# Attention into a SwiGLU block: q transposed in 32x32 blocks on VectorE, its loads in quarters of the partitions

## The chip, the cores and the metric

The kernel runs on one core of a Trainium2 chip. The metric is the device time of one execution in microseconds (us). The time before is the median of five runs, 1066.11 us (1065.39 to 1068.65). Traces come from the hardware profiler, one execution each.

The engines are TensorE (PE, matrix products and transposes through an identity), VectorE (DVE), ScalarE (ACT), GpSimd (POOL) and SyncE (SP), which in this kernel issues nearly all DMAs. SBUF has 128 partitions; PE writes to PSUM.

## The reference

```python
# q, k, v: (8, 8, 576, 64) = (batch B, head H, position S, D)
kv = np.einsum('bhsd,bhse->bhde', k, v)          # no softmax: one 64x64 matrix per head
out = np.einsum('bhsd,bhde->bhse', q, kv)
rms = np.sqrt(np.mean(out * out, axis=-1, keepdims=True) + 1e-06)
attn = out / rms * g_norm
x = attn.transpose(0, 2, 1, 3).reshape(4608, 512)
g = x @ w_gate                                     # (512, 1536)
h = g * (1.0 / (1.0 + np.exp(-g))) * (x @ w_val)
y = h @ w_out                                      # (1536, 512)
```

## The kernel before

The 4608 tokens are worked in nine blocks of 512 (NB = 9, BLK = 512, four tiles of 128). Block n ends batch n-1 and begins batch n, since a batch has 576 positions. `Att` holds the attention part of a block, `Ffn` the rest.

Attention. `load_kv` (L223) loads k and v for pairs of heads j = 0 to 3; `kv` (L255) multiplies them on PE, and one ACT copy (L261) and one DVE add make the 64x64 matrices of the batch. `load_q` (L238) loads two of the block's token tiles at a time with the tokens in the partitions: per partition eight runs, one for each head, of 64 numbers, 256 bytes. PE needs q with the head's dimension in the partitions, so `turn_q` transposes each tile in four 128x128 transposes on PE (L272) into PSUM, and ACT (L274) or DVE (L276) copies them out to `qt`: 16 transposes and four copies for each block. `product` (L292) multiplies qt by the kv matrices; `root` and `scale` do the norm, `turn_x` (L339) transposes the result, and `sums` makes the sums of its quarters (x and, from block 2 on, xi).

The FFN's products are done in the Strassen-Winograd manner, with seven products in place of eight, here in chains that accumulate in the PSUM tiles a, b and c. Block 0 is computed plainly (L861), since weights still arrive. Block 1 does one level in its up phase (`Up`, PE at L427). Blocks from DEEP = 2 on do two levels in the up phase (`Inner`, PE at L576), in 12 units; after nearly every product DVE adds the PSUM tile into a ring tile (L110), and at the end of four units h = silu(g) * v is made (L112, on POOL or, for the last, DVE). The down phase (`Down`, PE at L427) has one level: chains p = 1, 5, 6, 7, 2, 4, 3, each of 12 matmuls of 256 columns (two records each in the trace). Between two levels stand combined weights, which DVE makes in block 1 (`leaf_steps`); SP stores them to memory (L707 and L711, w<-r, w<-t, w<-xi), and streams them back in 51 chunks for each later block (`Stream.pump`, L655, t<-w) into a pool of nine tiles t.

The main loop runs, for each n: the up phase of block n, with the attention loads and kv products of block n+1 as fills between its units; `turn`, the transposes of q of block n+1; the first kv loads of block n+2; and the down phase, between whose products the steps of the attention of block n+1 (`half`, `turn_x`, `sums`) stand. The order of instructions on each engine comes from a scheduler that follows this order and the waits for tiles; pools of few buffers (ld four, t nine, ring r five, xi one, PSUM a one, b three, c two, m two) decide when a tile is free. The last up unit's product and the first Down product meet at the turn, where the transposes stand.

Two names recur: a deep block is one with n >= 2, and the seam is the place between its up and its down phase. All loads and stores named here go through SP's one queue, in order.

Of the kernel before, what the change touches and what calls it, by code (L numbers as in the profile page):

```python
# [8 lines left out]
F32 = mybir.dt.float32  # L9
# [5 lines left out]
P = 128  # L15
# [3 lines left out]
def kernel(  # L19
# [41 lines left out]
    nc = tc.nc  # L61

    B, H, S, D = q.shape
    NT, DM = out.shape
    FF = moe_w_gate.shape[1]
    T = 4
    BLK = P * T
# [3 lines left out]
    NS = DM // P  # L71
# [7 lines left out]
    def pool(name, bufs, **kw):  # L79
        return ctx.enter_context(tc.tile_pool(name=name, bufs=bufs, **kw))  # L80

    consts = pool("consts", 1)
    ld_pool = pool("ld", 4)
# [30 lines left out]
    def ring():  # L114

        return r_pool.tile([P, 4, BLK], F32, name="r")
# [67 lines left out]
    class Att:  # L184
# [29 lines left out]
        def load_kv(self, js):  # L214
            if self.n == B:
                return
            for j in js:
                hs = slice(2 * j, 2 * j + 2)
                for i, (tiles, src) in enumerate(((self.k, k), (self.v, v))):
# [6 lines left out]
                        )  # L226
                    tiles.append(t.rearrange("p h (t d) -> p h t d", t=KT))

        def load_q(self, i):
            if self.n == 1:  # L230
                tiles = [t_tile().rearrange("p a b -> p (a b)") for _ in range(2)]
            else:
                ld = ld_pool.tile([P, 2 * BLK], F32, name="ld")
                tiles = [ld[:, 0:BLK], ld[:, BLK : 2 * BLK]]
            for t in range(2):
                tile_ = tiles[t].rearrange("p (h d) -> p h d", h=H)
                for b, s0, p0, p1 in self.parts(2 * i + t):
                    nc.sync.dma_start(  # L238
                        out=tile_[p0:p1], in_=q[b, :, s0 : s0 + p1 - p0, :].rearrange("h p d -> p h d")
                    )  # L240
                self.q.append(tile_.rearrange("p (j u) d -> p j (u d)", u=2))
# [22 lines left out]
        def turn_q(self, i, pools=None):  # L264

            if i == 0:
                self.qt = ring().rearrange("p t (j c) -> p t j c", j=NS)
            for t in (2 * i, 2 * i + 1):
                pool = pools[t % 2] if pools else m_psum
                ps = pool.tile([P, NS, P], F32, name=pool.name[0])  # L270
                for j in range(NS):
                    nc.tensor.transpose(ps[:, j], self.q[t][:, j], ident)  # L272
                if t % 2 or self.n == 1 or self.n > DEEP:
                    nc.scalar.copy(out=self.qt[:, t], in_=ps)  # L274
                else:
                    nc.vector.tensor_copy(out=self.qt[:, t], in_=ps)  # L276
# [131 lines left out]
    DEEP = 2  # L408
# [261 lines left out]
    def t_tile(key=None):  # L670

        stream.held.append(key)
        return t_pool.tile([P, 2, 2 * P], F32, name="t")
# [206 lines left out]
    def weights(upto):  # L880
        nonlocal loaded, rounded
        while rounded < min(upto, len(pieces)):
            while loaded < min(rounded + 4, len(pieces)):
                load_w(*pieces[loaded])
                loaded += 1
            round_w(*pieces[rounded])
            rounded += 1

    def t2(place, b22, b11):

        sub(nc.vector, place, b22, place)
        add(nc.vector, place, place, b11)

    blocks = [Att(n) for n in range(NB)]
# [7 lines left out]
    for n in range(NB):  # L902
        ffn = Ffn(n, blocks[n])
        nxt = blocks[n + 1] if n + 1 < NB else None
        if n == 0:

            with tc.issue_after(scaled.ins):
                weights(2)
            ffn.plain_up(0, (0,))
            scaled = blocks[0].second()  # L910
            for f in range(NF):
                with tc.issue_after(scaled.ins):
                    weights(2 * (f + 2))
                if f == 1:
                    ffn.plain_up(1, (0,))
                    ffn.plain_up(0, (1,))
                ffn.plain_up(f, (1,)) if f == 1 else ffn.plain_up(f) if f else None
            weights(len(pieces))
            pairs = wo.rearrange("p (j e) d -> p e j d", e=2)
            t2(pairs[:, 0, :, HD:DM], pairs[:, 1, :, HD:DM], pairs[:, 0, :, 0:HD])  # L920
            nxt.room = x_pool.tile([P, 3, 7, P], F32, name="xi").rearrange("p a b c -> p (a b c)")
            nxt.load_kv(range(NS))
            for i in range(2):
                nxt.load_q(i)
            ffn.plain_end()
            nxt.kv(range(NS))
        else:

            def third():
                nxt.kv((0, 1))  # L930
                nxt.load_kv((2, 3))

            def two_thirds():
                nxt.kv((2, 3))
                for i in range(2):
                    nxt.load_q(i)

            ffn.up({4: third, 8: two_thirds} if nxt else {})
        if nxt:
            nxt.turn()  # L940
        if n + 2 < NB:
            blocks[n + 2].load_kv((0, 1))
        ffn.down(nxt.steps() if nxt else [])
        if n == 0:

            with tc.issue_after(nxt.halves[0].ins):
                for j in range(NP):
                    t2(wv[j][:, 0:2], wv[j][:, 2:4], wg[j][:, 0:2])
# [31 lines left out]
```

## Time and profile before

| | us |
|---|---|
| median of five runs | 1066.11 |
| lowest and highest | 1065.39, 1068.65 |
| profiled execution, its own time | 1068.65 |
| span of its trace | 1066.7 |
| PE busy in the span | 1040.1 (98%) |
| DVE busy | 699.0 (66%) |
| POOL busy | 366.4 (34%) |
| ACT busy | 244.9 (23%) |
| start of one deep down phase to the next | 111.76 |
| mean granted PE clock | 0.994 of full speed |

The span reaches from the first to the last instruction that the trace shows; 1.95 us of the profiled execution lie around it. Busy times of different engines overlap. In a line of the trace, `b<-x,t` says that the tile b is written from x and t, `x8` counts instructions, the first number is the start from the span's start and the second the time that the group takes; what stands in brackets is the idle time before it, and who ended it. Instructions of a group may overlap their neighbours, as PE's records are longer than their spacing. A row that ends in `383/622/3250` gives the least, median and most of a duration in ns, followed by the first and last start.

### The profile page before, as it was taken

To read this page: it belongs to the slowest core of one execution; us is meant where nothing else is said; L and a number is where in the kernel's file an instruction comes from. 1 tells how busy PE (TensorE), PEld (TensorE's weight loads), DVE (VectorE), ACT (ScalarE), POOL (GpSimd) and SP (SyncE) were. 2 spreads that over 40 slices of the span, in tenths; PEclk is the share of its full clock that TensorE was granted. 3 is DMA by queue.
4 is the path that set the end of the run, shared out by engine and by line. 5 is a ranking of instruction groups with operands and counts; after the bars stand their busy time and mean duration, and the time that the engine had idled before them with its cause. 6 is when DMAs were issued, how large, how long until landed. Compare 5 with 4: busy or idle time off the path is not lost.

```text
span 1066.7 us, 21799 instructions
## 1 busy us (share of the span) xinstructions
PE 1040.1 (98%) x8780; PEld 937.3 (88%) x8780; DVE 699.0 (66%) x1243; ACT 244.9 (23%) x392; POOL 366.4 (34%) x280
## 2 busy tenths in 40 slices
PE   5899999998999999999999999999999999999998
PEld 4644788877899989998999899989999899989997
DVE  2999596778556765576666666666667566755661
ACT  2666111221221211222112212121112211212110
POOL 0000453344025701462156305640455036602670
PEclk9999999998999999999999999999999999999999
DMA  9787103565468325741576247714782266126611
GB/s 239 221 265 231 57 12 105 160 172 162 158 209 240 112 71 193 238 147 61 163 244 169 83 128 229 220 53 129 225 230 70 90 202 189 50 80 202 189 31 40
DMA packets 154356, 161.87 MB, mean 152 GB/s; under 512 B 48400, under 2 KB 105104, under 8 KB 154256
## 3 DMA queue, kind: packets, MB, share of 16 engines
q1 hardware_dynamic: 154192, 160.48, 50.2%
q8 instruction: 70, 1.15, 0.5%
q14 instruction: 30, 0.25, 0.1%
q0 software_dynamic: 64, 0.00, 0.0%
HBM read 138.02 MB, written 22.41 MB: 150 GB/s over the span
## 4 chain that ended last, share of the span: by engine, by line
PE 92%; DVE 3%; DMA 2%; SPq 2%; POOL 1%; issue 1%; ACT 0%; DVEq 0%; POOLq 0%
PE b L576 25%; PE b L427 20%; PE c L576 12%; PE c L427 10%; PE a L576 6%; PE a L427 5%; PE c L861 4%; PE b L861 4%; PE m L255 2%; PE m L339 1%; PE m L292 1%; SPq L223 1%; PE b L292 1%; DVE r L111 1%; DMA ld<-in_moe_w_gate_dram 1%; PE b L272 1%
## 5 line engine op out<-in xcount | busy, mean ns | idle before, releaser
L110 POOL TENSOR_TENSOR r<-r 128x256 f32<-128x256 f32 (+1 forms) x105 | 110.2, 1055 | 365.7 <-DVE r L110 360.4
L110 DVE TENSOR_TENSOR r<-b,r 128x512 f32<-128x512 f32 (+1 forms) x273 | 162.1, 607 | 61.4 <-PE b L576 56.6
L110 DVE TENSOR_TENSOR r<-c,r 128x512 f32<-128x512 f32 (+1 forms) x177 | 108.9, 625 | 99.4 <-PE c L576 56.0
L111 POOL TENSOR_TENSOR t<-wo 128x512 f32<-128x512 f32 x81 | 113.1, 1423 | 162.1 <-DVE wo L110 108.4
L576 PE MATMUL b<-x,t 128*128 128x128 f32 x1092 | 151.2, 276 | 0.0
L576 PEld LDWEIGHTS b<-x,t 128*128 128x128 f32 x1092 | 136.0, 192 | 0.6
L110 DVE TENSOR_TENSOR r<-a,r 128x512 f32<-128x512 f32 (+1 forms) x99 | 62.6, 632 | 83.2 <-PE a L576 53.1
L112 POOL TENSOR_TENSOR h<-r 128x1024 f32<-128x1024 f32 (+1 forms) x40 | 81.5, 2053 | 93.2 <-DVE r L110 79.7
L576 PE MATMUL c<-xi,t 128*128 128x128 f32 x840 | 112.1, 275 | 0.0
L576 PEld LDWEIGHTS c<-xi,t 128*128 128x128 f32 x840 | 102.8, 192 | 0.0
L427 PE MATMUL b<-t,h 128*128 128x256 f32 x432 | 97.1, 381 | 0.0
L427 PE MATMUL b<-wo,h 128*128 128x256 f32 x432 | 96.2, 379 | 0.0
L427 PEld LDWEIGHTS b<-wo,h 128*128 128x128 f32 x432 | 81.4, 190 | 10.7
L427 PEld LDWEIGHTS b<-t,h 128*128 128x128 f32 x432 | 80.7, 190 | 11.0 <-issue 0.2
L590 ACT COPY r<-b 128x512 f32<-128x512 f32 x63 | 36.9, 586 | 219.1 <-PE b L576 184.9
L576 PE MATMUL b<-xi,t 128*128 128x128 f32 x588 | 79.7, 276 | 0.0
L576 PEld LDWEIGHTS b<-xi,t 128*128 128x128 f32 x588 | 72.4, 192 | 0.0
L576 PE MATMUL b<-x,wg 128*128 128x128 f32 x336 | 53.0, 280 | 0.0
L576 PE MATMUL b<-x,wv 128*128 128x128 f32 x336 | 51.2, 275 | 0.0
L427 PE MATMUL c<-t,s 128*128 128x256 f32 x216 | 48.9, 383 | 0.0
L427 PE MATMUL a<-wo,h 128*128 128x256 f32 x216 | 48.3, 379 | 0.0
L427 PE MATMUL c<-wo,h 128*128 128x256 f32 x216 | 48.1, 379 | 0.0
(129 smaller groups left out, 1649.8 us busy)
## 6 DMA issues: line engine op xcount, KB each, us to landing
t<-w SPq DMA_DIRECT2D x336, 256.0 KB, 2.9
out_dram<-r SPq DMA_DIRECT2D x18, 512.0 KB, 2.9
ld<-in_q_dram SPq DMA_DIRECT2D x29, 256.0 KB, 4.5
ld<-in_moe_w_gate_dram SPq DMA_DIRECT2D x12, 512.0 KB, 4.9
ld<-in_moe_w_val_dram SPq DMA_DIRECT2D x12, 512.0 KB, 5.1
ld<-in_moe_w_out_dram SPq DMA_DIRECT2D x12, 512.0 KB, 4.6
w<-t SPq DMA_DIRECT2D x36, 128.0 KB, 2.1
ld<-in_k_dram SPq DMA_DIRECT2D x26, 160.0 KB, 3.1
```

Source lines behind the costliest of these rows:

```text
L110: add = lambda e, o, a, b: e.tensor_tensor(out=o, in0=a, in1=b, op=OP.add)
L111: sub = lambda e, o, a, b: e.tensor_tensor(out=o, in0=a, in1=b, op=OP.subtract)
L112: mul = lambda e, o, a, b: e.tensor_tensor(out=o, in0=a, in1=b, op=OP.mult)
L223: nc.sync.dma_start(out=t[r * D : (r + 1) * D, :, 0 : m * D], in_=src[self.n, hs, s0 : s0 + m * D].rearrange("h (p t) d -> p h (t d)", t=m),)
L255: nc.tensor.matmul(self.kv_ps[r][u * D : (u + 1) * D, j, :], lhsT=self.k[j][rows, u, c, :], rhs=self.v[j][rows, u, c, :], start=(c == 0), ...
L272: nc.tensor.transpose(ps[:, j], self.q[t][:, j], ident)
L292: nc.tensor.matmul(self.ps[i][u][p : p + D, t, j, :], lhsT=self.qt[rows, 2 * i + t, j, p : p + D], rhs=kvs[b % 3][rows, j, :], start=True, ...
L339: nc.tensor.transpose(ps[:, e, t], xt[:, t, j + e], ident)
L427: nc.tensor.matmul(self.ps[name][:, e], lhsT=lhsT, rhs=rhs, start=first and (e, i) == (0, 0), stop=i == self.steps - 1, skip_group_check=True,
L576: nc.tensor.matmul(ps[:, i, f], lhsT=self.weight(o, p, f), rhs=self.operand(o, p), start=first and (i, f) == (0, 0), stop=True, skip_group ...
L590: nc.scalar.copy(out=dst, in_=ps)
L861: nc.tensor.matmul(t, lhsT=w[f // 2][:, i, P * (f % 2) : P * (f % 2 + 1)], rhs=x[:, i, of], start=(i == 0), stop=(i == NS - 1),)
```

## The change

For blocks from 2 on, q is loaded by a new function, `load_quarters`: for each pair of token tiles, each j of two and each quarter r of the partitions it loads 32 positions in 32 partitions by as many groups of 32 positions as belong to one batch, 32 numbers (128 bytes) to a run. A block's q takes 32 DMAs where it took four or five (16 where block 8 has one batch alone). `turn_q` then transposes in two VectorE instructions of 128x1024, which turn each 32x32 block in place, straight from SBUF to SBUF: with quarters of the columns in quarters of the partitions, that is the whole transpose. Sixteen PE transposes and four copies out of PSUM fall away per turn. qt lies in its ring tile in another order of dimensions. Blocks 0 and 1 keep PE transposes.

The loads of q of block n+2 move to the start of the down phase of block n, beside the first kv load. k and v are loaded and multiplied one j at a time, at units 2, 5, 8 and 11 of the up phase (2, 4, 8, 10 in block 1), where they were loaded and multiplied two at a time at 4 and 8; only the first j is loaded in the down phase before.

```diff
--- before.py
+++ after.py
@@ -226,7 +226,30 @@
                         )
                     tiles.append(t.rearrange("p h (t d) -> p h t d", t=KT))
 
+        def load_quarters(self, i):
+
+
+            ld = ld_pool.tile([P, 2 * BLK], F32, name="ld")
+            to = ld.rearrange("p (j g d) -> p j g d", j=2, d=P // 4)
+            cut = 2 * self.n
+            spans = [(self.n - 1, S - D * self.n, 0, cut), (self.n, 0, cut, BLK // 32)]
+            for j in range(2):
+                for r in range(4):
+                    h, d = divmod(r, 2)
+                    for b, s0, g0, g1 in spans:
+                        if g1 > g0:
+                            nc.sync.dma_start(
+                                out=to[32 * r : 32 * (r + 1), j, g0:g1],
+                                in_=q[b, 4 * i + 2 * j + h, s0 : s0 + 32 * (g1 - g0), 32 * d : 32 * (d + 1)].rearrange(
+                                    "(g p) d -> p g d", p=32
+                                ),
+                            )
+            self.q.append(ld)
+
         def load_q(self, i):
+            if self.n >= DEEP:
+                self.load_quarters(i)
+                return
             if self.n == 1:
                 tiles = [t_tile().rearrange("p a b -> p (a b)") for _ in range(2)]
             else:
@@ -264,13 +287,17 @@
         def turn_q(self, i, pools=None):
 
             if i == 0:
-                self.qt = ring().rearrange("p t (j c) -> p t j c", j=NS)
+                self.qt = ring().rearrange("p j (t c) -> p t j c", t=T)
+            if self.n >= DEEP:
+                to = self.qt[:, :, 2 * i : 2 * i + 2].rearrange("p t j c -> p j t c")
+                nc.vector.transpose(out=to.rearrange("p j t c -> p (j t c)"), in_=self.q[i])
+                return
             for t in (2 * i, 2 * i + 1):
                 pool = pools[t % 2] if pools else m_psum
                 ps = pool.tile([P, NS, P], F32, name=pool.name[0])
                 for j in range(NS):
                     nc.tensor.transpose(ps[:, j], self.q[t][:, j], ident)
-                if t % 2 or self.n == 1 or self.n > DEEP:
+                if t % 2 or self.n == 1:
                     nc.scalar.copy(out=self.qt[:, t], in_=ps)
                 else:
                     nc.vector.tensor_copy(out=self.qt[:, t], in_=ps)
@@ -926,20 +953,19 @@
             nxt.kv(range(NS))
         else:
 
-            def third():
-                nxt.kv((0, 1))
-                nxt.load_kv((2, 3))
-
-            def two_thirds():
-                nxt.kv((2, 3))
-                for i in range(2):
-                    nxt.load_q(i)
-
-            ffn.up({4: third, 8: two_thirds} if nxt else {})
+            def fill(j):
+                nxt.kv((j,))
+                if j + 1 < NS:
+                    nxt.load_kv((j + 1,))
+
+            at = (2, 5, 8, 11) if n >= DEEP else (2, 4, 8, 10)
+            ffn.up({a: (lambda j=j: fill(j)) for j, a in enumerate(at)} if nxt else {})
         if nxt:
             nxt.turn()
         if n + 2 < NB:
-            blocks[n + 2].load_kv((0, 1))
+            blocks[n + 2].load_kv((0,))
+            for i in range(2):
+                blocks[n + 2].load_q(i)
         ffn.down(nxt.steps() if nxt else [])
         if n == 0:
 
```

## The prediction

> **What bounds the kernel now.** I read the page's busy shares and the chain that ended last first:
>
> ```profile
> PE 1040.1 (98%) x8780; PEld 937.3 (88%) x8780; DVE 699.0 (66%) x1243; ACT 244.9 (23%) x392; POOL 366.4 (34%) x280
> PE 92%; DVE 3%; DMA 2%; SPq 2%; POOL 1%; issue 1%; ACT 0%; DVEq 0%; POOLq 0%
> ```
>
> TensorE is the bound, so work taken off it is worth its time, unless another engine then ends last. Next I looked at the place where the transposes stand, the turn from up to down of a deep block (n = 3 here; blocks follow each other every 111.76 us), on PE and on VectorE:
>
> ```profile
> 471.74 1.16 PE L576 MATMUL b<-x,t 128*128 128x128 f32 x8
> 472.73 0.60 PE L272 MATMUL m<-ident,ld 128*128 128x128 f32 x4
> 473.17 0.60 PE L272 MATMUL b<-ident,ld 128*128 128x128 f32 x4
> 473.61 0.60 PE L272 MATMUL m<-ident,ld 128*128 128x128 f32 x4
> 474.04 0.60 PE L272 MATMUL b<-ident,ld 128*128 128x128 f32 x4
> ...
> 472.99 0.69 DVE L110 TENSOR_TENSOR r<-b,r 128x512 f32<-128x512 f32 x1 [0.41 <-PE b L576]
> 473.78 2.52 DVE L112 TENSOR_TENSOR h<-r 128x1024 f32<-128x1024 f32 x2
> ```
>
> The 16 transposes occupy PE from 472.73 to 474.48 (start of the first Down product), 1.75 us, without a gap. Beside them DVE makes the last add and the last two products of h. How full both are, by windows (columns: PE, PEld, DVE, ACT and POOL busy, clock, DMA share, GB/s):
>
> ```profile
> 463.70:470.00 6.30, 6.30 (x58) 6.30 (x58) 4.91 (x10) 1.06 (x1) 5.15 (x6) 1.00 0.33 102
> 470.00:474.64 4.64, 4.64 (x42) 4.56 (x41) 3.62 (x5) 1.22 (x2) 2.33 (x1) 1.00 0.01 4
> 474.64:515.00 40.36, 40.36 (x311) 35.38 (x310) 26.93 (x46) 8.74 (x16) 8.91 (x6) 1.00 0.27 87
> 228.00:248.00 20.00, 15.70 (x57) 13.06 (x58) 14.30 (x35) 4.24 (x8) 5.33 (x5) 0.78 0.54 156
> ```
>
> PE has no idle time in the deep block and DVE has some. The last row is block 1, where the combined weights are also made: PE idles there at a lowered clock. Last, SyncE's queue at the end of block 1 and in a deep down phase:
>
> ```profile
> 272.61 2.87 SPq L711 DMA_DIRECT2D w<-xi  x3
> ...
> 473.80 1.25 SPq L223 DMA_DIRECT2D ld<-in_k_dram  x2
> 482.91 27.98 SPq L655 DMA_DIRECT2D t<-w  x9
> ```
>
> In block 1, SP issues its stores of weights back to back until 275.48; in a deep block it mostly waits for tiles.
>
> **PE transposes out: gain 10.5 us.** Seven turns lose 16 transposes each. Six stand in deep blocks (n = 2 to 7): 6 x 1.75 = 10.5 us, if the work behind can start that much sooner. The seventh (block 2's q, in block 1) has 6 of its 16 just before a PE gap of 3.38 us (ended by ACT); only the ten at 249.87 to 250.96, 1.1 us, lie on the path.
>
> **What is late next at the seam.** Down's p = 1 product has 12 matmuls of 0.432 us (24 records 0.216 apart); its last four need the last h. In the changed program the scheduler puts three Down matmuls ahead of the last Up group, so that group, its add and the h products move back by 3 x 0.432 = 1.30. The first h product then ends at 473.78 + 1.30 + 1.22 = 476.30; PE, free of transposes, reaches the ninth Down matmul at 474.48 + 8 x 0.432 - 1.75 = 476.19. It waits 0.11, six times.
>
> **VectorE transposes in: no gain; 1.5 us lost with the seam's wait, up to 15 us.** Fourteen new DVE instructions, two per turn, 128x1024 each, ten and four adds ahead of the h products. No row shows this operation. The nearest has the same shape and memory, 128x1024 f32 read and written in SBUF: 1.225 us (L112). Two take 2.45. The kv add, now at the eleventh unit instead of the eighth, joins them: 0.42 by the 128x256 adds, and DVE waits for an ACT copy ahead of it:
>
> ```profile
> DVE kv L110 <- ACT kv L261: 5.2, 5, 1.0
> ```
>
> That is 1.0 each. Queued behind both are the adds of the last units, and PE waits for these through the PSUM tiles that they free. So DVE gets 2.45 + 0.42 + 1.0 = 3.87 us more, and has 1.39 + 1.02 idle from 463.7 to 474.64 and the 1.30 by which the last group moves back, 3.71. It is short by 0.16; with the 0.11 above, 0.25 per seam (rounded), six times 1.5 us. There is no margin left: each 0.1 us by which a transpose exceeds 1.225 costs 6 x 2 x 0.1 = 1.2 us, a doubled one (2.45) 14.7. Below 1.225 at most the 1.5 come back. I take 1.225, as the nearest row. The evictions that go (26 on ACT of 0.59, 2 on DVE of 0.68) are beside the path. The first qt product, which reads the result, starts after the first Down chain.
>
> The Trainium skill ("Vector Engine (DVE) Microarchitecture Reference", section 3.8) has the 32x32 transpose sustain one element per cycle and lane; no run here shows it yet, and by it the price would be near the row's.
>
> **The loads on SP: between 0 and +12 us, taken +4.8, once.** q of blocks 2 to 8 now takes 32 DMAs per block (16 for block 8) of 32 partitions and 128-byte runs instead of 4 or 5: 177 more on SP. What an issue takes now (least, median and most, in ns):
>
> ```profile
> L238 SPq DMA_DIRECT2D ld<-in_q_dram x35: 383/622/3250, 0.7 to 800.6; - x35
> L223 SPq DMA_DIRECT2D ld<-in_k_dram x52: 595/602/1265, 98.9 to 764.2; - x52
> ```
>
> The least of L238 is that of 128 partitions, 0.383; L223's 0.602 is for 64 partitions, in steps of 0.67 with the gap. Thirty-two partitions are not shown; the nearest is 64, so 0.67 a step, 32 x 0.67 = 21.4 us per block. From below, 128 partitions give 0.43 a step; from above, if the halving again adds 0.22, 0.89. Each load also waits for the landing of the one eight before it: at 4.5 us to landing (the page's median for q), 0.56 a step at the least, so this wait is covered.
> - Deep blocks: issued after the remaining kv loads, from about 475 on, they end at 496.5. Queued behind them are the t<-w loads, 9 before the next up phase at 515.52 (9 x 0.37 = 3.3 us of issue and 2.9 to land), and stores at 511.15. That is late only if a step exceeds (515.52 - 6.2 - 475.1) / 32 = 1.07 us. Cost 0.
> - Block 1: block 3's 32 loads come ahead of the last 32 weight stores on a queue without air. They add 21.4, less four q(2) DMAs that move into down of block 0 (2.94) and four kv DMAs that move to later fills (2.7): 15.8 us. The last store is issued at 291.3 instead of 275.48 and lands 2.1 later, 293.4. Block 2's xi sums, whose tile these stores read, began at 286.01 and now wait for it; they last 4.34 and end at 297.7. PE first reads xi at 292.89: 4.8 us late. The 1.1 us of PE time saved and DVE's extra (2 x 1.225 - 2 x 0.685 = 1.1) in this block vanish in that wait. At 0.43 a step it is nothing, at 0.89 it is 12; each 0.05 is 1.6 us.
> - Bytes are unchanged and runs halve. When q is loaded now, with 256-byte runs, and when the weights stream, with 2 KB:
>
> ```profile
> 451.00:452.00 1.00, 1.00 (x11) 1.00 (x10) 0.21 (x1) 0.48 (x1) 0.00 (x0) 1.00 1.05 226
> 457.00:458.00 1.00, 1.00 (x11) 1.00 (x11) 0.69 (x1) 0.00 (x0) 1.00 (x1) 1.00 1.02 387
> ```
>
> If the rate halves again to 113 GB/s, a block's 1.05 MB takes 9.3 us, in a down phase where the DMA share is 0.27 of 40 us. Cost 0; moving it out of the full stretch of the up phase, where PE does not wait, gains 0.
>
> The rule that speaks against it is in the Trainium skill, "DMA: Bandwidth & Descriptors", Specifications: below 512 B a transfer is a read-modify-write and misses line rate. The two windows agree for 256 B (226 against 387 GB/s); by the rule the change is a loss on the queue's engines, by the windows one that nobody waits for.
>
> **kv one pair of heads at a time** (units 2, 5, 8, 11): the same matmuls and DMAs in smaller portions. Cost 0 on PE; its add is counted above.
>
> **Sum.** -10.5 + 1.5 + 4.8 = -4.2 us. The profiled execution took 1068.65 (span 1066.7 and 1.95 around it), the highest of five; so 1064.4 against it, and 1061.9 against the median, 1066.1, by which I state the numbers. About 0.2% (2.1 us) is what a measurement of this kernel can tell from no change.
>
> **Rivals.**
> - *Dear issues on SP.* A step of 32 partitions is over 0.75, say 0.9 to 1.1 us. For it: 64 partitions cost 0.22 more than 128. Against: the 64-partition loads of q and kv cost much the same though their runs differ, so a fixed price is as likely as a rising one. Block 1 then loses 12 to 18.5: -9.0 + 12 = +3 to -9.0 + 18.5 = +9.5, 1069 to 1075.6. It decides for slower from 0.80 a step (-9.0 + 4.8 + 32 x 0.13 = 0). Chance 0.27.
> - *Dear transposes on VectorE.* Over 1.4 us, say 2.45: -4.2 + 14.7 = +10.5, 1076.6; slower from 1.225 + 4.2 / 12 = 1.58. Against it is the equal shape of L112. Chance 0.12.
> - *The seam keeps the time.* Down's h ends last at the turn whatever PE does (today DVE ends it at 476.30, 1.8 us after PE has started Down), and PE waits for it. Half the gain stays: -5.25 + 4.8, about -0.4, 1065.7. Against it: today PE needs the last h only at 474.48 + 8 x 0.432 = 477.94. Chance 0.11.
> - *Forecast*, with a step of 0.43 to 0.75: -9.0 + 0 to -9.0 + 7.4, 1057.1 to 1064.5. Chance 0.50.
>
> **Numbers.** Forecast, SP, DVE and seam in this order: faster 0.46 + 0 + 0.03 + 0.04 = 0.53; same 0.04 + 0.07 + 0.02 + 0.05 = 0.18; slower 0 + 0.20 + 0.07 + 0.02 = 0.29. The range reaches down to the whole 10.5 with nothing given back, and up to a step of 1.05 (-4.2 + 32 x 0.38 = +8): 1055.5 to 1074.
>
> **What would show it.** Right: deep turns 1.5 us shorter (period about 110.3), no PE gap over 0.3 us at the first Down chain, DVE transposes of about 1.2 us, SP issues of about 0.6, and block 2's xi sums waiting for a w store until about 293. Wrong: transposes above 1.5 us, issues above 0.8 with block 2's up phase after 300, a deep up phase that waits for t<-w, or PE waiting for kv or q products.

## The result and the profile after

The changed kernel takes 1068.06 us (median of 23 runs, 1067.37 to 1070.80), against 1066.58 us before (median of 43): ratio 1.0019, 95% interval 1.0013 to 1.0024. It is slightly slower, where 1061.9 was forecast. Its profiled execution took 1069.35 us, its span is 1067.6. In the runs below, each ratio is against the kernel before on the same chip in the same rounds; the one profiled execution of a version differs from its median by up to 3.5 us (e6_kv_pairs), so stages are compared by traces and versions by ratios.

The page's busy shares, and the chain that ended last, after:

```profile
PE 1033.2 (97%) x8668; PEld 924.0 (87%) x8668; DVE 729.1 (68%) x1255; ACT 232.3 (22%) x366; POOL 369.5 (35%) x280
PE 81%; DVE 15%; SPq 1%; DMA 1%; issue 1%; ACT 0%; POOL 0%; DVEq 0%; POOLq 0%
```

PE has 112 instructions and 7 us less to do, and DVE now holds 15% of the chain instead of 3%. The next lines are the same seam as before the prediction (n = 3), on PE, DVE and POOL:

```profile
474.55 1.46 PE L454 MATMUL b<-wo,h 128*128 128x256 f32 x6
475.85 1.05 PE L603 MATMUL b<-x,t 128*128 128x128 f32 x8
476.74 3.62 PE L454 MATMUL b<-wo,h 128*128 128x256 f32 x15
...
477.01 0.69 DVE L110 TENSOR_TENSOR r<-b,r 128x512 f32<-128x512 f32 x1 [0.97 <-PE b L603]
477.73 2.39 DVE L112 TENSOR_TENSOR h<-r 128x1024 f32<-128x1024 f32 x2
480.88 0.69 DVE L111 TENSOR_TENSOR h<-s,h 128x512 f32<-128x512 f32 x1
...
481.71 8.99 POOL L111 TENSOR_TENSOR t<-wo 128x512 f32<-128x512 f32 x6 [6.66 <-DVE h L111]
```

The seam went nearly as forecast: three Down matmuls (six records) stand ahead of the last Up group, and DVE waits for PE (0.97). At the ninth Down matmul, where the last h is first read, two records of PE start 0.33 and 0.32 us after the one ahead of them instead of 0.216, so PE comes 0.22 us late there (the third PE line is cut off by the end of its window at 480 us). But the sums of h for which GpSimd waits end at 481.57, 7.02 us after the first Down matmul; in the kernel before they ended 3.27 after it (477.75 and 474.48). GpSimd's six differences t<-wo start only after these sums. What comes of that on DVE, and on PE 12 us further on, first in the kernel before, then in the changed one:

```profile
477.89 8.91 POOL L111 TENSOR_TENSOR t<-wo 128x512 f32<-128x512 f32 x6 [5.56 <-DVE h L111]
...
485.64 1.19 DVE L320 SCALAR_TENSOR_TENSOR a<-y 128x16 f32<-128x16 f32 x1
486.87 0.18 DVE L321 TENSOR_TENSOR a<-a,z 128x16 f32<-128x16 f32 x1
...
489.22 0.68 DVE L112 TENSOR_TENSOR r<-a,y 128x512 f32<-128x512 f32 x1
...
491.31 1.04 PE L339 MATMUL m<-ident,r 128*128 128x128 f32 x8
```

```profile
484.66 1.17 DVE L337 TENSOR_SCALAR z<-z 128x16 f32<-128x16 f32 x1
485.86 1.19 DVE L340 TENSOR_SCALAR y<-z 128x16 int32<-128x16 int32 x1
487.08 1.19 DVE L347 SCALAR_TENSOR_TENSOR a<-y 128x16 f32<-128x16 f32 x1
488.31 1.19 DVE L348 TENSOR_TENSOR a<-a,z 128x16 f32<-128x16 f32 x1
489.53 1.19 DVE L349 SCALAR_TENSOR_TENSOR y<-a,y 128x16 f32<-128x16 f32 x1
490.76 0.17 DVE L347 SCALAR_TENSOR_TENSOR a<-y 128x16 f32<-128x16 f32 x1
...
492.69 0.68 DVE L112 TENSOR_TENSOR r<-a,y 128x512 f32<-128x512 f32 x1
...
493.43 1.09 PE L366 MATMUL m<-ident,r 128*128 128x128 f32 x8 [0.77 <-DVE r L112]
```

The small operations of `root` on 128x16 numbers take 1.17 to 1.19 us each while GpSimd works (481.71 to 490.70), and 0.17 afterwards, the same instruction at L347 both times. Five are slow. The scale (L112) ends at 493.37, and `turn_x` on PE waits for it. In the kernel before, GpSimd's group was over at 486.80 and three small operations were slow; the last scale ended at 489.90, 1.41 us before PE came for it. Counted from the start of block 3's up phase (403.76 before, 406.00 after), PE now comes 1.06 us earlier, and the scale ends 1.23 later. The lists of waits (engine, line, releaser: total, times, longest), before and after:

```profile
PE m L339 <- DVE r L112: 4.9, 1, 4.9
```

```profile
PE m L366 <- DVE r L112: 9.9, 8, 4.9
```

Against the usual spacing of records (0.216 us) the wait costs 0.93 us, once in each deep block. Where the time lies, from the starts of the PE records in each trace (us):

| stretch | before | after |
|---|---|---|
| first PE record to block 0's down phase | 114.21 | 113.48 |
| block 0's down phase | 41.04 | 41.04 |
| from there to block 3's up phase (blocks 1 and 2, below "block 1") | 241.07 | 244.13 |
| block 3's to block 8's up phase | 555.78 | 554.56 |
| rest | 102.10 | 102.05 |
| one deep block inside | 111.76 | 111.64 |

So two things are to be explained: a deep block wins 0.12 us where 1.5 were forecast, and the stretch of block 1 loses 3 us.

### The profile page after: what moved, and what is told of

It reads as the page before. It is cut to its first block, busy times and chain, and to the rows that moved or that the text cites. A ratio compares the mean times of both kernels' runs of the same rounds, so it can differ in the third digit from the quotient of the medians.

```text
span 1067.6 us, 21774 instructions
## 1 busy us (share of the span) xinstructions
PE 1033.2 (97%) x8668; PEld 924.0 (87%) x8668; DVE 729.1 (68%) x1255; ACT 232.3 (22%) x366; POOL 369.5 (35%) x280
## 4 chain that ended last, share of the span: by engine, by line
PE 81%; DVE 15%; SPq 1%; DMA 1%; issue 1%; ACT 0%; POOL 0%; DVEq 0%; POOLq 0%
PE b L603 25%; PE b L454 14%; PE c L603 12%; PE c L454 6%; PE a L603 6%; PE a L454 4%; PE b L888 4%; PE c L888 4%; PE m L278 2%; PE m L366 2%; DVE h L111 2%; DVE h L112 1%; DVE xi L111 1%; DVE r L110 1%; DVE r L111 1%; DVE a L347 1%
## 5 line engine op out<-in xcount | busy, mean ns | idle before, releaser
L112 POOL TENSOR_TENSOR h<-r 128x1024 f32<-128x1024 f32 (+1 forms) x40 | 82.2, 2072 | 96.8 <-DVE r L110 74.0
L454 PE MATMUL b<-wo,h 128*128 128x256 f32 x432 | 98.7, 381 | 0.0
```

The costliest lines, as they stand in the source:

```text
L112: mul = lambda e, o, a, b: e.tensor_tensor(out=o, in0=a, in1=b, op=OP.mult)
L454: nc.tensor.matmul(self.ps[name][:, e], lhsT=lhsT, rhs=rhs, start=first and (e, i) == (0, 0), stop=i == self.steps - 1, skip_group_check=True,
```

## Experiments

**GpSimd's differences later (e1_late4, e2_before_late4).** `Down.turn_t` can wait for an instruction; the three differences of chain p = 4 now wait for the scale (`down` gets `nxt` as an argument for it).

```diff
-                    down.turn_t(4)
+                    down.turn_t(4, nxt.scaled if nxt else None)
```

> The changed kernel, with one thing more: GpSimd's three differences for Down's chain p = 4 (t<-wo) wait for the scale of the first half of the next block's attention. Theory (GpSimd): in the changed kernel GpSimd's six differences t<-wo run from 481.71 to 490.70 us, and five of the small VectorE operations of the norm take 1.19 us there instead of 0.17; so the scaled result comes late and PE waits 0.92 us for it ahead of turn_x, once in every deep block. With three of the differences put behind the scale, two or fewer small operations stay slow, the wait goes, and the time falls by 6 x 0.92 and up to 0.9 more in block 1: 1061.5 to 1063 us. Rival (the seam): VectorE is late because of the transposes and the later last Up group; the wait comes from there and hardly shrinks, 1067 to 1068.5. Rival (loads): no change, 1068.

Measured: 1069.12 us, ratio 1.0014 (1.0006 to 1.0023). The sum was missed, the mechanism held: a deep block takes 110.70 us, 0.94 less, and the waits of the deep blocks are gone. What was overlooked is block 0: its down phase takes 47.00 us instead of 41.04. There the moved differences begin only at 133.14, GpSimd then works without a break until 148.19, and all that time DVE makes weights beside it:

```profile
133.14 4.99 POOL L111 TENSOR_TENSOR t<-wo 128x512 f32<-128x512 f32 x3 [10.91 <-DVE r L112]
...
144.80 3.39 POOL L111 TENSOR_TENSOR t<-wg,wv 128x512 f32<-128x512 f32 x2
...
141.96 3.42 DVE L110 TENSOR_TENSOR wv<-wv,wg 128x512 f32<-128x512 f32 x2
145.31 3.42 DVE L111 TENSOR_TENSOR wv<-wv 128x512 f32<-128x512 f32 x2
148.65 1.28 DVE L110 TENSOR_TENSOR wv<-wv,wg 128x512 f32<-128x512 f32 x2
...
154.96 1.06 PE L366 MATMUL m<-ident,r 128*128 128x128 f32 x8 [4.08 <-DVE r L112]
```

The same pair of operations costs 3.42 us beside GpSimd and 1.28 alone, and PE waits 4.08 us for the second half's scale, which is queued behind them. What makes up the rest of the 5.96 us stays open.

> The kernel before with the same edit: GpSimd's differences for chain p = 4 wait for the scale. Theory (GpSimd): three small operations ran slowly here, but the scale ended ahead of PE's need, so there is nothing to win: 1066 to 1067 us. If the slow operations cost time by themselves whatever waits, it falls as in the changed kernel, by 5 us or more, to 1061.

Measured: 1073.83 us, ratio 1.0054 (1.0041 to 1.0067). Block 0 loses the same 5.95 us; a deep block stays at 111.76. In the kernel before nobody waited for the scale, so freeing it wins nothing there.

**The same edit from block 1 on (e5_late4_from1).**

```diff
-                    down.turn_t(4)
+                    down.turn_t(4, nxt.scaled if nxt and self.n else None)
```

> The changed kernel with GpSimd's three differences for chain p = 4 put behind the scale, in blocks 1 and on only. With the same edit in every block, a deep block took 110.70 us instead of 111.64 and the down phase of block 1 with what follows 2.7 us less, but the down phase of block 0 took 47.00 instead of 41.04. Theory (GpSimd): only that loss goes, so 1069.1 - 6.0, 1062 to 1064 against 1067.5 before; from the one trace, whose time was 2 us under its median, 1060 to 1062. If the deep gain came of the shifted start alone, it stays at 1067 to 1069.

Measured: 1062.13 us, ratio 0.9956 (0.9943 to 0.9968), inside the first forecast. A deep block takes 110.70 and block 1's stretch 241.45. GpSimd and DVE of n = 3:

```profile
479.10 5.31 POOL L111 TENSOR_TENSOR t<-wo 128x512 f32<-128x512 f32 x3 [6.67 <-DVE h L111]
487.80 3.72 POOL L111 TENSOR_TENSOR t<-wo 128x512 f32<-128x512 f32 x3 [3.39 <-DVE r L112]
...
483.25 1.19 DVE L340 TENSOR_SCALAR y<-z 128x16 int32<-128x16 int32 x1
484.48 0.18 DVE L347 SCALAR_TENSOR_TENSOR a<-y 128x16 f32<-128x16 f32 x1
```

Two small operations stay slow and the rest take 0.17 to 0.18. GpSimd gains too: its three differences take 3.72 us alone and 5.31 beside DVE.

**No transposes on VectorE (e7_copy_on_act).** The kernel leaves the transposition of q out.

```diff
-                nc.vector.transpose(out=to.rearrange("p j t c -> p (j t c)"), in_=self.q[i])
+                nc.scalar.copy(out=to.rearrange("p j t c -> p (j t c)"), in_=self.q[i])
```

> The changed kernel with the two 128x1024 transposes of VectorE replaced by two copies of the same tiles on ScalarE, so q is not transposed. It takes 2.5 us of VectorE per turn away and leaves the rest; the scheduler then puts no Down matmul ahead of the last Up group. Theory (GpSimd, started by the late end of h): h ends 1.3 us earlier against PE, GpSimd's differences start earlier and slow fewer small operations, and the wait of 0.92 us goes: 1061 to 1063. If VectorE's time counts by itself at the seam, more than that, 1058 to 1060; if neither, 1068.

Measured: 1064.74 us, ratio 0.9978 (0.9969 to 0.9987), above the 1061 to 1063 forecast, and the remainder lies in block 1. A deep block takes 110.73, as with GpSimd's edit, although GpSimd's group stays whole and four small operations are slow. Here no Down matmul stands ahead of the last Up group, h's sums end 4.88 us after the first Down matmul instead of 7.02, and PE finds the scale just ended. So the wait needs both, a late h and the slowing beside GpSimd; taking away either takes it away, and VectorE's transposes cost nothing beyond it: from the start of an up phase to the first qt product behind Down's first chain a deep block takes 74.93 us here and 74.94 in the changed kernel (76.00 before). Block 1's stretch stays at 244.65, so it has another cause.

**Everything but the transposes (e4_pe_transposes).** Both tests `self.n >= DEEP` that the change adds, in `load_q` and `turn_q`, become `self.n >= NB`.

> The changed kernel with every transpose of q on PE again and q loaded with the tokens in the partitions, but in the places of the change: q in the down phase two blocks ahead, k and v one pair of heads at a time. It prices the moved loads and the smaller portions alone. By the traces kv's matmuls cost 0.29 us more per block in four portions: seven blocks, 2 us, 1068.5 us against 1066.6 before. If the portions are free, 1066.6; if the seam's order costs on its own, more than 1069.

Measured: 1074.31 us, ratio 1.0059 (1.0046 to 1.0073), worse than expected. A deep block takes 112.42 us, 0.66 more than before, not 0.29. All of it lies ahead of the first qt product (76.66 us instead of 76.00). From block 3 on two copies per turn run on VectorE here that the kernel before has on ScalarE; they stand at the seam, and behind the first qt product the deep block takes as long as before (35.76 us). Where PE enters and leaves a portion of kv matmuls:

```profile
529.22 1.06 PE L603 MATMUL b<-xi,t 128*128 128x128 f32 x8
530.21 0.80 PE L278 MATMUL m<-ld 64*64 64x64 f32 x36
530.93 0.71 PE L603 MATMUL b<-x,t 128*128 128x128 f32 x4
531.48 0.61 PE L603 MATMUL c<-xi,t 128*128 128x128 f32 x4
```

The first group behind a portion is 0.1 longer and starts later against the portion's end; with what it costs on the way in, two more portions per block come to 0.66, 0.33 each. I had counted the spacing inside the portions alone. Set against the version of 110.70, the transposes are worth 1.72 us per turn, as forecast. Block 1's stretch takes 244.75 us here, 3.7 more than before, although no load of 32 partitions is left; at 0.66 us a block the portions of blocks 1 and 2 explain 1.3 of it at most.

**kv in pairs again (e6_kv_pairs, e8_kv_pairs_packed, e9_kv_packed_alone, e10_packed_from3).** One j has two heads; the texts below call two j, loaded and multiplied together, a pair. Such a pair needs all four load tiles, so q can't lie in two of them. The first run stands on e5_late4_from1 ("the run before it"), brings the pairs back and loads q late in the up phase.

```diff
+                nxt.load_q(0)
+            ffn.up({4: third, 8: two_thirds, 9 if n >= DEEP else 10: lambda: nxt.load_q(1)} if nxt else {})
...
-            blocks[n + 2].load_kv((0,))
-            for i in range(2):
-                blocks[n + 2].load_q(i)
+            blocks[n + 2].load_kv((0, 1))
```

> As the run before it in this list, but k and v in pairs of heads at units 4 and 8 as before the change, and the 32 loads of q in the up phase, 16 behind unit 8 and 16 behind unit 9. Theory (portions): each portion of kv matmuls costs PE 0.33 us on the way in and out, two fewer in each of seven blocks are 4.6 us: 4 to 5 us less than that run. Rival (SP): the 32 loads take 16.8 us of SP's queue and the remaining t<-w loads 6.3 us, of 23.6 us left in the up phase; the weights come late, PE waits on t, and it is no faster or slower by up to 5 us per block.

Measured: 1097.15 us, ratio 1.0287 (1.0271 to 1.0303), the rival's case:

```profile
PE b L603 <- DMA t<-w: 24.8, 5, 5.6
```

PE waits 5 us per block for weights that stand behind q's loads on SP. So of the two places tried the down phase is the better one for the small loads, with the portions as its price. Packing avoids both:

```diff
+    kvx_pool = pool("kvx", 1)
...
+                extra = kvx_pool.tile([P, 2 * KT * D], F32, name="kvx")
...
+                    ks = [ld[:, 0:w], ld[:, w : 2 * w]]
+                    vs = [ld[:, 2 * w : 3 * w], extra[:, x * w : (x + 1) * w]]
...
-            blocks[n + 2].load_kv((0,))
+            blocks[n + 2].load_kv((0, 1))
```

> The changed kernel with GpSimd's differences for chain p = 4 behind the scale from block 1 on, and with kv in pairs of heads at units 4 and 8 as before the change, while q stays in the down phase: one load tile holds both heads of k and one of v for a j, and a small tile of 2.5 KB per partition the other heads of v, so that a pair needs two load tiles and not four. Four more DMAs per pair. Theory (portions): 0.66 us per deep block come back, 4 to 4.6 us in all: 1062.1 - 4.5, 1057 to 1058.5. If the portions only filled time in which PE would have waited, it stays at 1062.

> The changed kernel with kv in packed pairs at units 4 and 8, and GpSimd's differences where the change has them. Theory: the 0.66 us per deep block of the portions come back, but PE then waits for the scale as before, and more, since PE's work up to there is the same and the wait hangs on h and GpSimd: 1068 - 4.5 = 1063 to 1064. If the wait swallows the gain, 1068.

Measured: 1066.62 us, ratio 0.9998 (0.9989 to 1.0007), with GpSimd's edit, and 1067.45, ratio 1.0001 (0.9993 to 1.0010), without. A deep block takes 110.09 and 111.01: each 0.61 to 0.63 less than its counterpart, so portions and wait add up, and the price of the portions is seen a second time without e4_pe_transposes. But block 1's stretch took 247.09 and 245.40, which gave the gain away; both totals miss their first forecasts. With packing from block 3 on:

> As the version with packed pairs of kv and GpSimd's differences behind the scale from block 1 on, but the pairs are packed from block 3 on only; block 2's kv goes one j at a time as in the change. With packing in every block a deep block took 110.09 us against 110.70 without, but block 1's down phase with what follows took 160.37 against 154.52. Theory (portions in deep blocks are 0.66 us each, the rest was block 1's own order): five or six deep blocks keep 0.6 us, block 1 is that of the unpacked version: 1062.1 - 3, 1058.5 to 1060. If packing itself delays the blocks, 1062 or more.

Measured: 1063.78 us, ratio 0.9960 (0.9946 to 0.9974); deep blocks near 110.1, block 1's stretch 246.12, so the forecast is missed in block 1 again. The packed loads of block 3, issued in block 1's down phase, cost there 4.7 us against 241.45 without them.

**Block 1 (e3_block2_on_pe, e11_q3_late).** First, block 2's q on PE (`self.n > DEEP` in both tests).

> The changed kernel, but block 2's q loaded with the tokens in the partitions (five DMAs in the down phase of block 0) and transposed on PE; from block 3 on as in the change. Theory (block 1 is bound by VectorE): the two transposes of 1.24 us and the wait of 0.87 us ahead of them leave VectorE's queue there, two copies of 0.69 come in; the PE gap of 6.2 us shrinks, 1.1 us of PE transposes come back: 1065.5 to 1067.5. Rival (SP): block 1 is late because block 3's 32 loads hold up the weight stores; they stay, so 1068 or a little more.

Measured: 1072.28 us, ratio 1.0041 (1.0028 to 1.0053), and block 1's stretch 246.40. My theory fell: VectorE's transposes are no loss there, with PE's in their place it is 2.3 us worse. Next, block 3's 32 loads moved behind the stores of weights:

```diff
+            if n != 1:
+                for i in range(2):
+                    blocks[n + 2].load_q(i)
+        ffn.down(nxt.steps() if nxt else [])
+        if n == 1:
             for i in range(2):
                 blocks[n + 2].load_q(i)
-        ffn.down(nxt.steps() if nxt else [])
```

> The changed kernel with block 3's 32 q loads issued after block 1's down phase has been written out, so that the last weight stores of block 1 are not behind them on SP. Rival (SP), the term of 4.8 us in the prediction: the stores end some 15 us earlier, block 2's sums no longer wait, and 2 to 3 us come back, 1065 to 1066. Theory: the sums begin where VectorE's queue lets them, at 292.65 us, after the last store has landed, so nothing comes back: 1068 within 0.7; a loss if the t<-w loads come late.

Measured: 1067.44 us, ratio 0.9998 (0.9989 to 1.0006); block 1's stretch 241.63, 2.5 us less. The gain is the rival's (2.2 us by the two ratios), its mechanism isn't shown. SP in the changed kernel, and the first of block 2's xi sums in the changed kernel and in this run:

```profile
247.78 16.80 SPq L241 DMA_DIRECT2D ld<-in_q_dram  x32
...
285.96 1.57 SPq L738 DMA_DIRECT2D w<-xi  x3
...
292.65 1.09 DVE L110 TENSOR_TENSOR xi<-x 128x896 f32<-128x896 f32 x1
```

```profile
286.62 1.09 DVE L110 TENSOR_TENSOR xi<-x 128x896 f32<-128x896 f32 x1
```

The sums start 6 us earlier. In the changed kernel DVE shows no wait directly ahead of them, and the last store, issued at 287.10, landed at 288.80 us, 3.85 before them; DVE is busy with work that came late. It does wait for stores earlier, ahead of sums of combined weights (1.47 us at 272.16), but e5_late4_from1 has that wait too (1.71), with a stretch of 241.45. Whether the late work came by such waits or by the scheduler's order, which moved too, was not separated. Nor can block 3's loads be the whole loss. The longest gap of PE in block 1 grew from 3.38 to 6.17 us and ends before SP issues the first of them (247.78); in e4_pe_transposes, which has none of them, it is 7.05 us. Before and after:

```profile
243.47 3.75 PE L427 MATMUL b<-x,t 128*128 128x256 f32 x8 [3.38 <-ACT r L478]
```

```profile
244.84 3.75 PE L454 MATMUL b<-x,t 128*128 128x256 f32 x8 [6.17 <-ACT r L505]
```

All of PE's waits for this copy by ScalarE take 5.7 us before and 7.8 after. Why they grew stays open.

**Both, and all (e12_late_and_q3, e13_all).** The edits of e5_late4_from1 and e11_q3_late together, and with the packed pairs from block 3 on.

> The changed kernel with two things more: GpSimd's differences for chain p = 4 behind the scale from block 1 on (1062.1 us alone), and block 3's q loads behind block 1's down phase (down phase of block 1 and what follows 154.25 us alone, against 156.33 in the changed kernel and 154.52 with the GpSimd edit alone). Theory: both take away the same wait for the scale in block 1, and the loads only the rest, so 1061 to 1062.5. If SP's loads cost 2 us of their own there, the sum holds: 1060 or less.

> As the run before it in this list, with kv in packed pairs of heads from block 3 on. Theory: 0.6 us less in each of five or six deep blocks, 2.3 to 3.6 us in all: 1058 to 1060. If the additional loads of the packed pairs delay block 1 again (159.0 us with the GpSimd edit and packing, against 154.52 without), 1062 to 1064.

Measured: 1060.76 us, ratio 0.9938 (0.9924 to 0.9951), and 1057.73 us, ratio 0.9912 (0.9899 to 0.9926). Block 1's stretch takes 239.33 and 239.26: from 244.13, the loads (2.50) and GpSimd (2.68) nearly add, to 4.80. With block 3's q loads out of the way, packed pairs no longer delay block 1. The last version beats both kernels by 0.9 and 1.1%; its deep block takes 110.09 us, 1.67 less than before the change.

## Why the prediction was wrong

- **PE transposes, -10.5:** right in size (1.72 to 1.75 per deep turn), but little of it arrived: the five deep periods from block 3's to block 8's up phase shrank by 1.22 us together.
- **"What is late next at the seam":** this is the step that failed. I followed h to its first consumer, the ninth Down matmul, where PE indeed waits little (0.22 us), and stopped. The next place is `turn_x`, 14 us further on, behind h's sums, the square sums, `root` and the scale, all on DVE, with GpSimd's differences released by the same sums. "The first qt product starts after the first Down chain" was true and not the question. Before, the scale ended 1.41 us ahead of PE; the change moved PE 1.06 us forward and the scale 1.23 back, 0.88 more than that slack, and 0.06 pass from the scale's end to PE's start. Price 0.93 per deep block.
- **"kv one pair of heads at a time ... Cost 0 on PE":** the second failed term, 0.66 per deep block. The sum of a deep block is -1.75 + 0.66 + 0.93 = -0.16, measured -0.12.
- **VectorE transposes:** the duration was right:

```profile
L293 DVE STREAM_TRANSPOSE r<-ld x14: 1221/1233/1245, 235.3 to 916.5; 128x1024 f32<-128x1024 f32 x14
```

  1.233 us against 1.225 taken. Of the 0.25 us per seam, 0.22 is seen at the ninth Down matmul, but the net loss did not occur: up to the first qt product a deep block takes 74.94 us with that wait and 74.93 in e7_copy_on_act without it.
- **SP, +4.8 once:** block 1 lost 3.1 us, and 2.5 of them come back when block 3's loads move (e11_q3_late). That this is near the forecast is luck. The step was too dear; an issue of 32 partitions takes 0.450 at the median, and 32 take 16.80, 0.525 a step instead of 0.67. By the same sum that leaves 4.8 - 32 x 0.145 = 0.2 us, and the wait it names, block 2's xi sums for the last store, isn't in the trace of the changed kernel. What makes block 1 late stays open. No deep block waited for t<-w, as forecast.

```profile
L241 SPq DMA_DIRECT2D ld<-in_q_dram x208: 311/450/1664, 121.3 to 812.0; - x104
```

- **Rivals:** "Dear issues" and "dear transposes" are out by these two rows. "The seam keeps the time" came nearest (1065.7), with the right engine and the wrong place: not h, but the scale behind it. It had no term for the portions.

The Trainium skill ("SBUF — State Buffer", Who interferes with whom) says that a VectorE instruction with two SBUF inputs contends with a GpSimd instruction that reads SBUF, and that the one that comes second waits. The rows of L347 to L349, which have two inputs, agree: 0.17 becomes 1.19 on DVE, and 3.72 becomes 5.31 on GpSimd. L337 and L340 have one tensor input and are slowed as well, which that sentence doesn't cover. The rows alone carry the explanation.

## What to carry to other kernels

Taking work off the bounding engine brings it earlier to every later place where it can wait: follow each chain that feeds it to the next places where it meets the engine, not only to the first, and add the slack at each. Small VectorE operations can be dear beside GpSimd work (here 1.19 us instead of 0.17); where somebody waits for a chain of them, it is worth moving that work, and worth looking at what it then runs beside, as block 0 showed. Cutting a piece of work into smaller portions on a full engine has a price per portion; read it from the spacing around one that exists.

## What was not expected of the hardware

- A VectorE operation on 128x16 numbers takes 0.17 us alone and 1.17 to 1.19 us beside GpSimd's 128x512 differences (changed kernel, n = 3); a pair of 128x512 operations takes 1.28 and 3.42 us (e1_late4).
- Each further portion into which the same 64x64 kv matmuls are cut costs PE 0.31 to 0.33 us (two cost 0.66 in e4_pe_transposes, 0.61 and 0.63 by e8_kv_pairs_packed and e9_kv_packed_alone).
- SP issues a DMA of 32 partitions in 0.450 us (median, changed kernel), where 64 partitions take 0.60 and 128 at the least 0.38 (kernel before): the price rose from 128 to 64 and not from 64 to 32.
- A 32x32 block transpose of 128x1024 numbers on VectorE takes 1.233 us, as long as an elementwise product of that shape (1.225 us).
